# Attention, expert and gated expert on one core: the order of issue set by the kernel's own event list, and attention beside the first expert by whole blocks

## The chip, the core and the metric

One core of a Trainium2 chip runs the whole program. The metric is the device time of one execution in microseconds. TensorE (PE) multiplies, PEld is its weight load, VectorE (DVE), ScalarE (ACT) and GpSimd (POOL) work element by element, SyncE (SP) issues most transfers. Products are summed up in eight banks of 128 x 512 fp32 each.

## What is computed

Attention of 2 batches, 8 heads, 768 positions, 64 values per head, each position seeing 96 positions behind it and 8 global ones; then an expert (silu) of width 2048, then a gated expert of width 1536, over 1536 tokens of 512 values:

```python
scores = scale * np.matmul(q, k.transpose(0, 1, 3, 2)) + bias     # bias: -slope * distance
scores = np.where(keep, scores, -1000000000.0)                    # keep: global or local
a = np.exp(scores - np.max(scores, axis=-1, keepdims=True))
a = a / (np.sum(a, axis=-1, keepdims=True) + 1e-09)
x = np.matmul(a, v)                                               # to tokens x 512
h = x @ w_in
x = (h * (1.0 / (1.0 + np.exp(-h)))) @ w_out
gate = 1.0 / (1.0 + np.exp(-(x @ w_gate)))
out = gate * (x @ w_val) @ w_out2
```

## The kernel before

**Precision.** A product of the experts is made of three on TensorE (`mm3`): each operand is kept as a high and a low part, and high x high, high x low and low x high go into one bank. The weights lie in memory as 64-bit floats. Each tile w0, w1, ... of 128 x 512 weights is loaded raw (`stage`), turned into fp32 in `u` (L156 on ScalarE, a shift L157 and two merges L158 and L161 on VectorE), and cut into its parts (L169 on ScalarE, the subtraction L170 on VectorE). There are 16 tiles w0 to w15 until attention ends, then 24. The tiles come in the order in, in, out, out for each pair of columns of the first expert.

**Attention.** A block is 128 queries of one batch; there are 12, each with four head pairs (`n` counts head pairs). Of a head pair TensorE makes two transposes of queries and keys (`emit_T`, L342, evacuated to `kt` by L353 or L355), the scores (`emit_QK`, L379: 256 columns, or 128 in a batch's first block), four transposes of the probabilities (`emit_PT`, L430, evacuated to `pt` by L434), and PV products (`emit_PV`, L451). Scores and PV are products in fp32, which the trace shows as two records each. In between stand the score operation on VectorE (L394, adds the mask and takes the maximum), the exponentials on ScalarE (L401), two small operations on the sums (L407, L408) and the division, on GpSimd (L413) or, for early blocks, in half on VectorE (L411). When a block's PV is done, `take` writes it to X: the high part by ScalarE (L468), the low part by VectorE (L469). X is cut into three groups x0, x1, x2 of four blocks.

**Stages.** `run_att` does six units of two head pairs, with fillers (bf16 products of a zero tile, L897) put in by hand: 11 ahead, 3 behind each step. `window` runs the rest of attention beside the first expert's first two groups, along `PLAN`: ten entries, each with a pair of columns, a stretch of tokens of a group and a number of attention units (20 in all, two for a block). An entry's products x,w go to banks 5 and 6, the silu makes g (L525, L526, L530 and L532), and its output products g,w are issued during the next entry, into bank 7, evacuated to `acc` by L589 or L591. `phase_rest` does what is left of both experts.

**What sets the order.** A scheduler of the tile framework orders the instructions by its own simulation; from the 16th head pair on, the scores and PV of a unit are tied in the order written. A unit of `att_units` is: scores of two head pairs and PV of the two of a block earlier; then by turns a transpose of probabilities and one of queries and keys. Banks: scores 0 and 1, probabilities 2, PV 3, transposes of queries and keys 4.

Of the kernel before, what the change touches and what calls it, by code (L numbers as in the profile page):

```python
# [11 lines left out]
I32 = mybir.dt.int32  # L12
# [12 lines left out]
TIE = 16  # L25
# [3 lines left out]
N_GLOB = 8  # L29


@with_exitstack
def attn_moe_moe2_kernel(
# [14 lines left out]
    nc = tc.nc  # L48
    B, H, S, D = q.shape
# [15 lines left out]
    stage_p = fast.enter_context(tc.tile_pool(name="stage", bufs=3))  # L65
    u_p = fast.enter_context(tc.tile_pool(name="up", bufs=2))
    g_p = fast.enter_context(tc.tile_pool(name="gp", bufs=4))
    e_p = fast.enter_context(tc.tile_pool(name="ep", bufs=2))
# [10 lines left out]
    nc.gpsimd.memset(pad, 0.0)  # L79
    W = [main.tile([128, 2, 512], F32R, name=f"w{n}") for n in range(16)]  # L80

# [71 lines left out]
    def to_f32(st, raw):  # L153
        lw, hw = raw[:, :, 0], raw[:, :, 1]
        ui = st.bitcast(I32)
        nc.scalar.activation(out=st, in_=hw.bitcast(F32), func=AF.Copy, scale=2.0 ** -112)  # L156
        nc.vector.tensor_scalar(ui, ui, 3, None, op0=ALU.logical_shift_left)  # L157
        nc.vector.scalar_tensor_tensor(  # L158
            out=ui, in0=lw, scalar=29, in1=ui, op0=ALU.logical_shift_right, op1=ALU.bitwise_or
        )  # L160
        nc.vector.scalar_tensor_tensor(  # L161
# [3 lines left out]
    def split_w(n):  # L165
        w = W[n % 24]
        st = u_p.tile([128, 512], F32, tag="u", name="u")
        to_f32(st, stages.pop(n))
        nc.scalar.activation(out=w[:, 0, :], in_=st, func=AF.Copy)  # L169
        nc.vector.tensor_tensor(w[:, 1, :], st, w[:, 0, :].bitcast(F32), ALU.subtract)  # L170

    def load_raw(st, s):
        o = st.rearrange("p f t -> p (f t)")
        if len(s.shape) == 3:
            o = o.rearrange("p (a f) -> p a f", f=256)
        nc.sync.dma_start(out=o, in_=s)

    def dma_w(n):
        st = stage_p.tile([128, 512, 2], I32, tag="stage", name="stage")
# [34 lines left out]
    qk_p = att.enter_context(tc.tile_pool(name="qkp", bufs=2))  # L214
    v_p = att.enter_context(tc.tile_pool(name="vp", bufs=3))
    t_p = att.enter_context(tc.tile_pool(name="tp", bufs=5))
    pt_p = att.enter_context(tc.tile_pool(name="ptp", bufs=3))
# [3 lines left out]
    ssum = [ap1.tile([128, 2], F32, name=f"ssum{i}") for i in range(4)]  # L221

    def load_n():
        raw = ap1.tile([128, 2, 2], I32, name="nraw")
        nc.sync.dma_start(out=raw[:, 0, :], in_=n_global.bitcast(I32).partition_broadcast(128))
        nc.scalar.dma_start(out=raw[:, 1, :], in_=n_local.bitcast(I32).partition_broadcast(128))
        return raw

    def make_n(raw):
        f = ap1.tile([128, 2, 2], F32, name="nf")  # L230
        neg = ap1.tile([128, 2, 1], F32, name="nneg")
        nc.vector.tensor_copy(f, raw)
# [729 lines left out]
```

## Time and profile before

| | us |
|---|---|
| median of 3 runs (682.02 to 682.70) | 682.52 |
| the profiled execution | 681.75 |
| its span in the trace | 680.0 |
| TensorE busy | 667.6 (98%) |
| VectorE busy | 374.2 (55%) |
| ScalarE busy | 277.9 (41%) |
| GpSimd busy | 84.6 (12%) |
| first expert product starts at | 41.40 |
| first product of `phase_rest` that stands alone starts at | 201.11 |

Busy shares are means over stages with different limits. In timeline rows, runs of one kind of instruction stand together; the step from the start of one run to the start of the next is the cost of the run, since the duration printed overlaps the next one's beginning. On VectorE and TensorE alike an instruction's record is longer than its share of the engine. A bracket at the end of a row says how long the engine stood idle ahead of it, and who ended that.

### The profile page before, as it was taken

Reading aid. Unit: us, or ns where it says so; the run is one execution under the profiler, and the core shown is the slowest. Engines: PE = TensorE matmul, PEld = TensorE weight load, DVE = VectorE, ACT = ScalarE, POOL = GpSimd, SP = SyncE. Lnnn points to the kernel's source line nnn. Section 1 sums busy time; section 2 is a strip of 40 time slices with the busy share of each in tenths; the row PEclk is TensorE's granted clock in tenths of the full one; section 3 lists DMA queues with packets and bytes.
Section 4 is the critical chain, followed back from the end, with each engine's and each line's share of the span. In section 5 each row is a group of like instructions: output and inputs, shape, how many; then the busy total and the mean of one; then the engine's idle time right before and its main releaser. Section 6 shows DMA issues by size and latency. Waiting matters only on the chain.

```text
span 680.0 us, 9291 instructions
## 1 busy us (share of the span) xinstructions
PE 667.6 (98%) x3463; PEld 540.1 (79%) x3463; DVE 374.2 (55%) x869; ACT 277.9 (41%) x594; POOL 84.6 (12%) x167
## 2 busy tenths in 40 slices
PE   9999999999999999999999999999999999999996
PEld 7577886777778888888888888888888888888884
DVE  5999975635549999652499941311783311312212
ACT  3797865555546565332366521111452111111110
POOL 4255564343220000000000000000000000000000
PEclk9899999999999999999999999999999999999999
DMA  8666652210004554400025430000250000100101
GB/s 215 174 171 164 171 150 63 48 33 17 17 2 128 182 155 153 125 0 1 24 70 169 141 94 1 0 1 0 63 155 1 1 0 1 62 1 1 62 1 67
DMA packets 65301, 49.05 MB, mean 72 GB/s; under 512 B 39648, under 2 KB 60128, under 8 KB 65248
## 3 DMA queue, kind: packets, MB, share of 16 engines
q1 hardware_dynamic: 64032, 48.11, 24.6%
q8 instruction: 29, 0.48, 0.3%
q10 hardware_dynamic: 1216, 0.26, 0.2%
q14 instruction: 24, 0.20, 0.1%
HBM read 45.22 MB, written 3.15 MB: 71 GB/s over the span
## 4 chain that ended last, share of the span: by engine, by line
PE 93%; DVE 5%; ACT 1%; issue 0%; DVEq 0%
PE bank L505 54%; PE bank L684 14%; PE bank L682 13%; PE bank L379 4%; PE bank L451 3%; PE bank L430 2%; PE bank L897 2%; PE bank L342 1%; DVE t L394 1%; DVE acc L591 1%; DVE w L170 0%; DVE u L158 0%; DVE u L161 0%; DVE acc L703 0%; ACT t L401 0%
## 5 line engine op out<-in xcount | busy, mean ns | idle before, releaser
L505 PE MATMUL bank<-x,w 128*128 128x512 f32 (+1 forms) x1488 | 347.1, 384 | 0.0
L505 PEld LDWEIGHTS bank<-x,w 128*128 128x128 f32 x1488 | 272.6, 188 | 54.4 <-issue 0.8
L542 DVE TENSOR_TENSOR sg<-sg,bank 128x512 f32<-128x512 f32 x36 | 24.7, 687 | 162.5 <-PE bank L505 162.5
L684 PE MATMUL bank<-w,g 128*128 128x512 f32 x432 | 103.9, 389 | 0.0
L684 PEld LDWEIGHTS bank<-w,g 128*128 128x128 f32 x432 | 81.1, 188 | 16.8
L682 PE MATMUL bank<-g,w 128*128 128x512 f32 x384 | 92.4, 389 | 0.0
L682 PEld LDWEIGHTS bank<-g,w 128*128 128x128 f32 x384 | 72.1, 188 | 15.0
L539 ACT ACTIVATE sg<-bank 128x512 f32<-128x512 f32 x36 | 21.6, 599 | 117.3 <-PE bank L505 117.1
L543 ACT ACTIVATE g<-sg 128x512 fp32r<-128x512 f32 x36 | 22.8, 632 | 90.5 <-DVE sg L542 90.5
L156 ACT ACTIVATE u<-stage 128x512 f32<-128x512 f32 x68 | 45.8, 675 | 26.5 <-DVE w L170 26.0
L505 PE MATMUL bank<-g,w 128*128 128x512 f32 (+1 forms) x240 | 53.9, 360 | 2.6 <-DVE acc L591 1.3
L413 POOL TENSOR_SCALAR t<-t,ssum 128x256 f32<-128x256 f32 (+1 forms) x88 | 48.3, 564 | 60.2 <-DVE ssum L408 25.6
L169 ACT ACTIVATE w<-u 128x512 fp32r<-128x512 f32 x68 | 42.5, 629 | 26.2 <-PE bank L505 10.4
L170 DVE TENSOR_TENSOR w<-u,w 128x512 fp32r<-128x512 f32 x68 | 46.9, 692 | 11.4 <-ACT w L169 11.3
L401 ACT ACTIVATE t<-t,nm_all 128x256 f32<-128x256 f32 (+1 forms) x96 | 46.1, 484 | 17.0 <-DVE nm_all L394 17.0
L161 DVE SCALAR_TENSOR_TENSOR u<-stage,u 128x512 int32<-128x512 int32 x68 | 48.2, 709 | 0.3
L158 DVE SCALAR_TENSOR_TENSOR u<-stage,u 128x512 int32<-128x512 int32 x68 | 46.8, 688 | 0.7
L505 PEld LDWEIGHTS bank<-g,w 128*128 128x128 f32 x240 | 38.0, 189 | 10.5 <-DVE acc L591 3.8
L394 DVE CUSTOM_DVE_ANT_0 t<-bank,mask 128x256 f32<-128x256 f32 (+1 forms) x96 | 33.7, 395 | 16.6 <-PE bank L379 15.8
L530 ACT ACTIVATE g<-sg 128x512 fp32r<-128x512 f32 x48 | 30.3, 631 | 22.2 <-DVE sg L529 12.0
L529 DVE SCALAR_TENSOR_TENSOR sg<-sg,bank 128x512 f32<-128x512 f32 x32 | 21.9, 683 | 27.9 <-ACT sg L528 27.9
L528 ACT ACTIVATE sg<-bank 128x512 f32<-128x512 f32 x32 | 19.1, 596 | 39.6 <-PE bank L505 39.2
(91 smaller groups left out, 516.4 us busy)
## 6 DMA issues: line engine op xcount, KB each, us to landing
stage<-in_moe_w_out_dram SPq DMA_DIRECT2D x28, 512.0 KB, 3.6
stage<-in_moe_w_in_dram SPq DMA_DIRECT2D x16, 512.0 KB, 3.7
stage<-in_moe_w_gate_dram SPq DMA_DIRECT2D x12, 512.0 KB, 3.5
stage<-in_moe_w_val_dram SPq DMA_DIRECT2D x12, 512.0 KB, 3.5
v<-in_v_dram SPq DMA_DIRECT2D x12, 256.0 KB, 3.5
out_dram<-acc SPq DMA_DIRECT2D x12, 256.0 KB, 2.0
qk<-in_k_dram SPq DMA_DIRECT2D x11, 256.0 KB, 3.6
qk<-in_q_dram SPq DMA_DIRECT2D x11, 256.0 KB, 3.8
```

Of the source, the lines that this page charges most:

```text
L156: nc.scalar.activation(out=st, in_=hw.bitcast(F32), func=AF.Copy, scale=2.0 ** -112)
L158: nc.vector.scalar_tensor_tensor(out=ui, in0=lw, scalar=29, in1=ui, op0=ALU.logical_shift_right, op1=ALU.bitwise_or)
L161: nc.vector.scalar_tensor_tensor(out=ui, in0=hw, scalar=-2 ** 31, in1=ui, op0=ALU.bitwise_and, op1=ALU.bitwise_or)
L169: nc.scalar.activation(out=w[:, 0, :], in_=st, func=AF.Copy)
L170: nc.vector.tensor_tensor(w[:, 1, :], st, w[:, 0, :].bitcast(F32), ALU.subtract)
L394: nc.vector.tensor_tensor_reduce(t[:, e, 0:w], sp[e], mask[e][:, m0:m0 + w], op0=ALU.add, op1=ALU.min, scale=-c, scalar=3.0e38, accum_out= ...
L401: nc.scalar.activation(out=t[:, e, 0:w], in_=t[:, e, 0:w], func=AF.Exp, scale=-1.0, bias=nm_all[:, gi, 2 * p + e:2 * p + e + 1], accum_out ...
L413: nc.gpsimd.tensor_scalar(t[:, e, 0:w], t[:, e, 0:w], ss[:, e:e + 1], 1.0, op0=ALU.mult, op1=ALU.mult)
L505: nc.tensor.matmul(ps, wl[(slice(None), a) + wsl], xl[(slice(None), b) + xsl], start=(first and j == 0), stop=(last and j == len(order) - 1),)
L530: nc.scalar.activation(out=gt[:, 0, :], in_=sg, func=AF.Copy)
L682: nc.tensor.matmul(yb[d], w[:, a, sl], gt[:, b, :], start=st, stop=en)
L684: nc.tensor.matmul(yb[d], gt[:, a, sl], w[:, b, :], start=st, stop=en)
```

## The change

Operations are no longer handed to the framework at once. `en.tensor`, `en.vector` and so on record them (`Op`) with the regions that they read and write; `link` finds who must come after whom; `order` picks by a list schedule on its own event model (the next engine that can start, among operations that can start within 0.02 us the earliest written), and `issue` hands them over in that order, which the framework keeps. `together` makes a group that isn't broken up. Fillers are put where the model sees TensorE idle before the window. `issue` is called twice: at the window's end and at the end. The tiles of stage, u, g, sg, qk, v, t and pt are fixed rings in place of pools (pt has four in place of three).

In the window, attention goes by whole blocks: `block_units` issues the scores of a block's four head pairs and the PV of the block before as one group, then four transposes of queries and keys, then four of probabilities, spread over the entries of `PLAN`. Banks: scores 0 to 3, probabilities 0 to 3, PV and transposes of queries and keys share 4, outputs 7, then 7 and 4 in the last entry, and 7, 4 and 3 behind the window.

```diff
+SEM = {"tensor": 0.2, "vector": 0.03, "scalar": 0.03, "gpsimd": 0.03, "sync": 0.05}
+TURN = {"fr": 0.095, "fc": 0.097, "tr": 0.095, "tc": 0.097, "rf": 0.192, "cf": 0.148, "rt": 0.247, "ct": 0.203,
+        "rc": 0.195, "cr": 0.147, "tf": -0.082}
...
+    def order(self, filler):
...
+        while any(cand.values()):
+            best = None
+            for e, cs in cand.items():
+                if cs:
+                    at = [(max(free[e], max(m.ready for m in g)), p, i, g) for p, i, g in cs]
+                    s = min(a[0] for a in at)
+                    a = min((a for a in at if a[0] <= s + 0.02), key=lambda a: a[1:3])
+                    if best is None or a[0] < best[0]:
+                        best = a[0], e, a
+            at, e, (_, prio, i, g) = best
+            cand[e].remove((prio, i, g))
+            if e == "tensor" and self.filling:
+                self.filling = not g[0].stop_fill
+                if self.filling:
+                    done += [filler] * max(0, int((at - free[e] - 0.15) / 0.115))
...
+    def issue(self, filler):
+        self.on = False
+        self.link()
+        done = self.order(filler)
+        self.first = len(self.ops)
+        with self.tc.manual_schedule():
+            for o in done:
+                if isinstance(o, Op):
+                    getattr(getattr(self.nc, o.eng), o.meth)(*o.args, **o.kw)
+                else:
+                    o()
...
+    def block_units(b0):
+        def run(b):
+            n = b * NP
+            with en.together():
+                sp = [emit_QK(n + p) for p in range(NP)]
+                for p in range(NP):
+                    emit_PV(n - NP + p)
+            take(n - 1)
+            for p in range(NP):
+                soft(n + p, sp[p], p)
+
+        n = b0 * NP
+        yield lambda n=n: emit_PT(n - 2)
+        yield lambda n=n: emit_T(n + 2)
+        yield lambda n=n: emit_PT(n - 1)
+        yield lambda n=n: emit_T(n + 3)
+        for b in range(b0, NBLK + 1):
+            n = b * NP
+            yield lambda b=b: run(b)
+            for p in range(NP):
+                yield lambda n=n + NP + p: emit_T(n)
+            for p in range(NP):
+                yield lambda n=n + p: emit_PT(n)
...
-            yb = bk["Y"][0]
+            yb = bk["Y"][(d // 2 if two else d) % len(bk["Y"])]
...
+        au_all = list(block_units(n0 * 2 // NP))
+        share, used = 0, 0
         for g, c, n, col0, slots in PLAN:
-            au = list(att_units(n0, n0 + slots))
-            n0 += slots
+            share += slots
+            upto = min(share * (len(au_all) - 1) // (SLOTS - 1), len(au_all))
+            au = au_all[used:upto]
+            used = upto
+            if share == SLOTS:
+                bk["Y"] = [bank[7], bank[4][:, 0:512]]
...
         for j, u in enumerate(att_units(n0, n1)):
             u()
-            warm_up(3)
             unit()
...
         run_att(0, START)
-        bk.update(SA=[bank[0]], SB=[bank[1]], PT=[bank[2]], PV=[bank[3]], T=[bank[4]],
-                  H=[bank[5], bank[6]], Y=[bank[7]])
+        en.stop_fill = True
+        bk.update(SA=[bank[0], bank[2]], SB=[bank[1], bank[3]], PT=bank[0:4], PV=[bank[4]],
+                  T=[bank[4][:, 0:256], bank[4][:, 256:512]], H=[bank[5], bank[6]], Y=[bank[7]])
         prev = window(START)
+        assert not deferred
+        en.issue(filler)
```

First place, VectorE ahead of the second block's write to x0 (u and stage are weight work, t and nm_all scores, kt and ssum attention). Before:

```order
L161 SCALAR_TENSOR_TENSOR u_729<-stage_459,u_729 128x512
L157 TENSOR_SCALAR u_771<-u_771 128x512
L353 TENSOR_SCALAR kt3_131<-bank4_80 128x256
L408 RECIPROCAL ssum1_137<-ssum1_137 128x2
L407 TENSOR_SCALAR ssum2_138<-ssum2_138 128x2
L158 SCALAR_TENSOR_TENSOR u_771<-stage_569,u_771 128x512
L407 TENSOR_SCALAR ssum3_139<-ssum3_139 128x2
L408 RECIPROCAL ssum2_138<-ssum2_138 128x2
L394 ISA t_627,nm_all_92<-bank0_76,mask0_126 128x256
L394 ISA nm_all_92 128x1
L394 ISA t_630,nm_all_92<-bank0_76,mask0_126 128x256
```

The row behind these is the write. After, the rows up to it and the one behind it (every recorded operation stands on L235):

```order
L235 ISA t4_137,nm_all_80<-bank0_64,mask0_113 128x256
L235 ISA nm_all_80 128x1
L235 ISA t4_137,nm_all_80<-bank1_65,mask1_114 128x256
L235 ISA nm_all_80 128x1
L235 TENSOR_TENSOR w2_85<-u0_102,w2_85 128x512
L235 TENSOR_SCALAR ssum2_125<-ssum2_125 128x2
L235 TENSOR_SCALAR u1_103<-u1_103 128x512
L235 RECIPROCAL ssum2_125<-ssum2_125 128x2
L235 TENSOR_TENSOR x0_75<-bank3_67,x0_75 128x4x128
L235 SCALAR_TENSOR_TENSOR u1_103<-stage0_99,u1_103 128x512
```

Before, the sixth weight tile is begun ahead of the write; now the fourth has had its shift alone.

Second place, TensorE in the window, a unit of attention beside expert products (g,w is an output product into bank 7, x,w one of the next entry). Before:

```order
L505 MATMUL bank7_83<-g_944,w7_102 128x256 x3
L379 MATMUL bank0_76<-kt1_129 128x256
L379 MATMUL bank1_77<-kt1_129 128x256
L379 MATMUL bank0_76<-kt0_128 128x256
L379 MATMUL bank1_77<-kt0_128 128x256
L342 MATMUL bank4_80<-ident_84,qk_686 128x128 x2
L505 MATMUL bank5_81<-x0_87,w0_95 128x256
L505 MATMUL bank6_82<-x0_87,w4_99 128x256
L430 MATMUL bank2_78<-ident_84,t_796 128x128 x4
L505 MATMUL bank5_81<-x0_87,w0_95 128x256 x11
```

After, the end of a block's run (eight scores and six PV rows stand ahead of these) and what follows it:

```order
L235 MATMUL bank4_68<-pt0_138,v2_132 64x128 x2
L235 MATMUL bank4_68<-pt0_138,v1_131 64x128 x2
L235 MATMUL bank7_71<-g0_104,w2_85 128x256 x3
L235 MATMUL bank6_70<-x0_75,w4_87 128x256 x3
L235 MATMUL bank7_71<-g0_104,w3_86 128x256 x3
L235 MATMUL bank6_70<-x0_75,w4_87 128x256 x3
L235 MATMUL bank4_68<-ident_72,qk0_128 128x128 x4
L235 MATMUL bank0_64<-ident_72,t0_133 128x128 x4
L235 MATMUL bank4_68<-ident_72,qk0_128 128x128 x4
L235 MATMUL bank6_70<-x0_75,w4_87 128x256 x6
L235 MATMUL bank7_71<-g0_104,w2_85 128x256 x3
```

Transposes into bank 4 now follow twelve expert products behind the PV run that filled it.

Third place, TensorE at the window's end, the output products. Before, all into bank 7:

```order
L505 MATMUL bank7_83<-g_2221,w11_106 128x512 x3
L451 MATMUL bank3_79<-pt_2234,v_1780 64x128 x2
L451 MATMUL bank3_79<-pt_2234,v_1955 64x128 x2
L451 MATMUL bank3_79<-pt_2207,v_1780 64x128 x2
L451 MATMUL bank3_79<-pt_2207,v_1955 64x128 x2
L505 MATMUL bank7_83<-g_2298,w14_109 128x512 x3
L505 MATMUL bank7_83<-g_2304,w15_110 128x512 x3
```

After:

```order
L235 MATMUL bank4_68<-g0_104,w10_93 128x512 x3
L235 MATMUL bank4_68<-g1_105,w11_94 128x512 x3
L235 MATMUL bank7_71<-g2_106,w14_97 128x512 x3
L235 MATMUL bank7_71<-g3_107,w15_98 128x512 x3
L235 MATMUL bank4_68<-g2_106,w14_97 128x512 x3
L235 MATMUL bank4_68<-g3_107,w15_98 128x512 x3
L235 MATMUL bank3_67<-g2_106,w14_97 128x512 x3
L235 MATMUL bank3_67<-g3_107,w15_98 128x512 x3
L235 MATMUL bank7_71<-g2_106,w14_97 128x512 x3
```

The outputs of an entry now stand in a row and change banks.

## Rows read from the trace of the kernel before

**Rows 1.** The page, the chain that ended last, by engine.

```profile
PE 93%; DVE 5%; ACT 1%; issue 0%; DVEq 0%
```

**Rows 2.** Windows: length, busy us and records of each engine; clock, DMA share, GB/s.

```profile
20.00:41.00 21.00, 19.72 (x132) 12.60 (x131) 19.70 (x78) 17.80 (x54) 6.73 (x17) 0.92 0.70 182
50.00:90.00 40.00, 39.07 (x328) 33.35 (x328) 39.93 (x108) 31.90 (x79) 22.33 (x29) 1.00 0.62 167
201.00:673.00 472.00, 472.00 (x2084) 390.64 (x2082) 234.97 (x393) 153.59 (x250) 0.00 (x0) 1.00 0.18 57
```

**Rows 3.** Timeline ahead of the first expert product: start, us, engine, line, operation.

```profile
38.22 0.41 DVE L157 TENSOR_SCALAR u<-u 128x512 int32<-128x512 int32 x1
38.55 0.41 DVE L353 TENSOR_SCALAR kt<-bank 128x256 f32<-128x256 f32 x1
...
39.01 0.68 DVE L158 SCALAR_TENSOR_TENSOR u<-stage,u 128x512 int32<-128x512 int32 x1
39.61 0.15 DVE L407 TENSOR_SCALAR ssum<-ssum 128x2 f32<-128x2 f32 x1
...
39.78 0.42 DVE L394 CUSTOM_DVE_ANT_0 t<-bank,mask 128x256 f32<-128x256 f32 x1
...
40.50 0.69 DVE L469 TENSOR_TENSOR x<-bank,x 128x512 fp32r<-128x512 f32 x1
...
41.40 0.37 PE L505 MATMUL bank<-x,w 128*128 128x256 f32 x1
```

**Rows 4.** Timeline of TensorE ahead of the first scores, at 8.95.

```profile
7.00 2.02 PE L897 MATMUL bank<-warm 128*128 128x256 bf16 x17
```

**Rows 5.** Timeline of TensorE in the window: attention pieces.

```profile
112.35 0.66 PE L451 MATMUL bank<-pt,v 128*64 128x128 f32 x8
112.94 0.44 PE L430 MATMUL bank<-ident,t 128*128 128x128 f32 x2
...
140.38 0.70 PE L379 MATMUL bank<-kt 64*128 64x256 f32 x4
141.01 1.09 PE L451 MATMUL bank<-pt,v 128*64 128x128 f32 x16
...
168.20 0.60 PE L430 MATMUL bank<-ident,t 128*128 128x128 f32 x4
168.56 1.87 PE L505 MATMUL bank<-x,w 128*128 128x512 f32 x7
...
173.56 1.09 PE L451 MATMUL bank<-pt,v 128*64 128x128 f32 x16
174.58 0.66 PE L430 MATMUL bank<-ident,t 128*128 128x128 f32 x4
175.17 1.13 PE L379 MATMUL bank<-kt 64*128 64x256 f32 x8
176.23 0.44 PE L342 MATMUL bank<-ident,qk 128*128 128x128 f32 x2
176.43 1.64 PE L505 MATMUL bank<-g,w 128*128 128x512 f32 x6
```

**Rows 6.** A wait in the timeline; waits of 41 to 201 us: total, times, longest.

```profile
64.61 1.69 PE L505 MATMUL bank<-g,w 128*128 128x256 f32 x12 [0.88 <-DVE acc L589]
...
PEld bank L505 <- DVE acc L591: 3.8, 9, 0.6
```

**Rows 7.** Line L170 up to 100 us: durations, first and last start.

```profile
L170 DVE TENSOR_TENSOR w<-u,w x16: 666/680/886, 19.6 to 87.8; 128x512 fp32r<-128x512 f32 x16
```

**Rows 8.** Timeline: a block's write behind a PV run.

```profile
188.84 0.60 ACT L468 ACTIVATE x<-bank 128x512 fp32r<-128x512 f32 x1 [0.40 <-PE bank L451]
...
189.47 0.69 DVE L469 TENSOR_TENSOR x<-bank,x 128x512 fp32r<-128x512 f32 x1 [0.98 <-ACT x L468]
```

**Rows 9.** Windows with the granted clock ahead of DMA share and GB/s.

```profile
28.66:32.07 3.41, 3.41 (x17) 2.71 (x16) 3.41 (x12) 1.50 (x7) 1.28 (x3) 0.50 0.44 146
104.65:109.33 4.68, 3.68 (x34) 2.49 (x34) 2.81 (x11) 2.52 (x7) 0.57 (x3) 1.00 0.52 112
```

More of the change, by code (lines that the diff above doesn't have):

```diff
@@ L1 @@
[L1 removed]
+from contextlib import ExitStack, contextmanager
+from itertools import cycle
 import concourse.bass as bass
@@ L24 @@
 HA = 8
-TIE = 16
+SLOTS = sum(r[-1] for r in PLAN)
 NEG = 1.0e30
@@ new lines, in region @@
+def region(a):
+    ps, pc = list(a.ap)[0]
+    free = [(st, c) for st, c in list(a.ap)[1:] if c > 1]
+    p0, f0 = (a.offset // ps, a.offset % ps) if ps else (0, a.offset)
+    free.sort(key=lambda e: -abs(e[0]))
+    width = 1
+    while free and abs(free[-1][0]) <= width:
+        st, c = free.pop()
+        width = max(width, (c - 1) * abs(st) + width)
+    runs = [f0]
+    for st, c in free:
+        runs = [r + k * st for r in runs for k in range(c)]
+    return a.name, a.space, p0, p0 + pc, tuple((r, r + width) for r in sorted(runs))
@@ L32, in attn_moe_moe2_kernel, with ring @@
+def ring(pool, shape, dt, name, n):
+    return cycle([pool.tile(shape, dt, name=f"{name}{i}") for i in range(n)])
 @with_exitstack
@@ L307, in load_qk @@
         b, s0 = gi // BLK, gi % BLK * 128
-        t = qk_p.tile([128, 2, H, D], F32, tag="qk", name="qk")
+        t = next(qk_r)
         if gi == 0:
@@ L387, in soft @@
         w = 128 if i == 0 else 256
-        t = t_p.tile([128, 2, 256], F32, tag="t", name="t")
+        t = next(t_r)
         t_t[n] = t
@@ L427, in emit_PT @@
         ps = bk["PT"][n % len(bk["PT"])]
-        for e in range(2):
-            for c in range(nk):
-                nc.tensor.transpose(
-                    ps[:, (e * nk + c) * 128:(e * nk + c + 1) * 128], t[:, e, c * 128:(c + 1) * 128], ident
-                )
-        pt = pt_p.tile([128, 512], F32, tag="pt", name="pt")
-        nc.scalar.activation(out=pt[:, 0:256 * nk], in_=ps[:, 0:256 * nk], func=AF.Copy)
+        with en.together():
+            for e in range(2):
+                for c in range(nk):
+                    en.tensor.transpose(
+                        ps[:, (e * nk + c) * 128:(e * nk + c + 1) * 128], t[:, e, c * 128:(c + 1) * 128], ident
+                    )
+        pt = next(pt_r)
+        en.scalar.activation(out=pt[:, 0:256 * nk], in_=ps[:, 0:256 * nk], func=AF.Copy)
         pt_t[n] = pt
@@ L892, in attn_moe_moe2_kernel, with filler @@
     main2 = {}
-    warm = ap1.tile([128, 256], BF16, name="warm")
-    def warm_up(n):
-        for _ in range(n):
-            nc.tensor.matmul(bank[5][:, 0:256], warm[:, 0:128], warm, start=True, stop=True)
+    def filler():
+        nc.tensor.matmul(
+            bank[5][:, 0:256].rearrange("p (a b) -> p a b", a=2), warm, warm2, start=True, stop=True
+        )
     with ExitStack():
         nc.vector.memset(warm, 0.0)
-        warm_up(11)
+        make_identity(nc, ident)
+        en.begin()
         load_qk(0)
-        make_identity(nc, ident)
         make_iota()
@@ L923, in attn_moe_moe2_kernel @@
         wst["gap"] = 7
+        bk["Y"] = [bank[7], bank[4], bank[3]]
+        en.begin()
         phase_rest(prev)
         flush()
+        en.issue(filler)
     fast.close()
```

515 lines of the change are left out of this document (341 added, 174 removed).

## The prediction

> **What bounds the kernel now.** I read the chain that ended last first: 93% of the span is TensorE and 5% VectorE [rows 1]. That share is a mean, so the busy time by stretches comes next. From 201 us to 673 TensorE has no idle time, and 2084 products in 472.00 us make 0.2265 us for a product of 512 columns [rows 2]. The change issues the same products there on the same weights with VectorE busy for half the stretch, so nothing can come off it. All that can move lies in the first 201 us: the attention start up to the first expert product, and the window in which attention runs beside the first expert. In the start, between 20 and 41 us, VectorE is busy for 19.70 of 21 us, and between 50 and 90 for 39.93 of 40, while TensorE is busy for 39.07 of these 40 [rows 2]. So two engines are nearly full in the window, and a gain on one can stop at the other. Then I read the timeline of VectorE ahead of the first expert product, the timeline of TensorE through attention, and the waits.
>
> **The start.** The first expert product starts at 41.40, right behind VectorE's write of the second attention block at 40.50 + 0.69 [rows 3]. VectorE is busy almost without a break until then, so its order decides. Counted in the two orders ahead of this write: before, 6 shifts of L157, 11 merges of L158 and L161 and 4 subtractions of L170 (weight work), and 18 score operations of 256 columns. After, 4, 6, 3 and 16. Start to start a shift takes 0.33 (38.22 to 38.55), a merge 0.60 (39.01 to 39.61), a score operation about 0.35 (39.78 to 40.50 for two) [rows 3]. I give the subtraction 0.60 too, for it has the merge's size. What leaves the queue ahead of the write is 2 x 0.33 + 5 x 0.60 + 0.60 + 2 x 0.35 = 5.0 us. Against it: 50 fillers stand ahead of the first transpose of queries and keys where about 28 stood. A filler takes about 0.11 (17 in the 1.95 us from 7.00 to 8.95) [rows 4], so the first transpose is about 2.4 later. But before the change TensorE did only fillers from 7.00 until the first score product at 8.95 could start [rows 4], so this slack covers most, and I charge 0.5. The start gives -4.5. Bounds: 0, if it is TensorE's own chain of transposes and products that sets the write, and -5.0.
>
> **Turns on TensorE.** In the window TensorE changes between expert products, score products (kt), transposes and PV products (pt, v). One run of each for two head pairs: PV 173.56 to 174.58 is 1.02, transposes of probabilities 0.59, scores 1.06, transposes of queries and keys 0.20, together 2.87 up to 176.43 [rows 5]. The other two transposes of such a piece stand among expert products: 0.36 (168.20 to 168.56) [rows 5] and, as the row above, 0.20. A piece is 3.43, and a block, two pieces, 6.86. A run has a fixed part: scores for one head pair take 0.63 (140.38 to 141.01) and for two 1.06; PV of one takes 0.59 (112.35 to 112.94) and of two 1.02 [rows 5]. Each further pair costs 0.43. So a whole block in one run costs 1.06 + 2 x 0.43 = 1.92 for scores and 1.02 + 0.86 = 1.88 for PV, and with four transposes of each kind among expert products 4 x 0.36 + 4 x 0.20 = 2.24 the block is 6.04. The gain is 0.82 a block. Nine blocks have both runs in the window, and the last block's PV alone becomes one run from two (-0.16): -7.5. Some work comes into the window that stood ahead of it, for ahead of the first expert product the order has two head pairs of scores (0.86) and two of query transposes (0.40) less, and half a pair of probability transposes (0.18) more: +1.1. Turns give -6.4. Bounds: -7.5 and -4, if every second transpose comes to stand beside an attention run, as it did before at 0.59.
>
> **Waits for bank 7.** All output products of the first expert go through one bank. At 64.61 TensorE waits 0.88 for its evacuation, and weight loads wait 3.8 us in nine other places for the same reason [rows 6]. The new order puts other products between an output and the next one on bank 7, and for the last two groups of outputs turns over banks 7 and 4, then 7, 4 and 3. That gives -4.7; bounds -1 (the 0.88, if weight loads had cover) and -4.7.
>
> **Given back to VectorE.** From the end of the second block's write at 41.2 to the end of the last weight that the window needs, VectorE takes 47.3 us (last subtraction at 87.8, and its 0.68) [rows 7]. In the new order more stands between these two points, counted: 1 shift, 5 merges, 1 subtraction, 2 score operations of 256 columns and 8 of 128, 4 evacuations of kt, 9 small sums, 3 evacuations of bank 7 and 2 block writes. At the prices above, 0.6 for each full-width one, 0.33 for a kt, 0.2 for a narrow score and 0.1 for a small sum, that is 0.3 + 3.0 + 0.6 + 0.7 + 1.6 + 1.3 + 0.9 + 1.8 + 1.2 = 11.4, so 58.7 in all, from 36.7 to about 95.4. TensorE's rows up to the seventh evacuation, with the prices above and about half of 0.2265 for a product of 256 columns, come to some 53 us after the first product at 36.9: 90. TensorE would stand there up to 5.4 us for weights. Some products that need no new weight can stand in the hole, so I charge +4; bounds 0 and +5.4. This takes the place of the start's gain, in part: VectorE's total work is the same, and only its order changes.
>
> **New waits.** PV and the transposes of the next block's queries now share bank 4, so the transposes stand behind the block's write. With idle engines this write takes 1.32 us (ScalarE at 188.84, VectorE's end at 190.16) [rows 8]; queued behind the transposes on TensorE is everything, since its order is fixed. Between a run and its first transpose the order has 12 or 6 products of 256 columns early (1.4 or 0.7 us) and 8 to 9 of 512 later (about 2). With VectorE full in the first half, three or four blocks can lose about 0.5: I charge +2, bounds 0 and +4. Scores in four banks and the fourth pt tile take waits away rather than add them, and since TensorE shows no wait for either in the rows, I cost them at nothing.
>
> **Sum.** -4.5 - 6.4 - 4.7 + 4 + 2 = -9.6 against the profiled execution's 681.75, or 672.2. Its time is 0.77 below the median of the runs shown, 682.52; added back, 672.9.
>
> **The rivals.** *Both costs are covered*: -4.5 - 6.4 - 4.7 = -15.6, 666.9. For it speaks that the new order is planned against engine models with durations close to these rows; against it, VectorE's full 40 us [rows 2]. *VectorE sets the pace until its weights are done* at about 95: then all that is saved earlier is given back, and what is left is turns behind that point (five blocks and the last PV, 4.3) and some 3 of the waits, less 1 for new ones: -6.3, 676.2. *Bank 4 takes it all*: if the write waits in VectorE's queue 1 us longer than I assume in each of nine blocks, +9 cancels the gain: 682. *Slower, by the clock*: between 28.66 and 32.07 the granted clock was 0.50, that is 1.2 GHz in place of 2.4, after a stretch with only scores and transposes and a wait [rows 9]. That cost half of 3.41, 1.7 us. A whole block now runs 3.8 us of scores and PV with no expert product between. If each of nine such runs brought one fall, it would cost 15.3 and the time would be 688; it decides from the sixth fall on. Against it: from 104.65 to 109.33 there is almost only attention on TensorE and 1.00 us without work, and the clock stayed at 1.00 [rows 9].
>
> The Trainium skill, "TensorE: Matmul & The Clock Gate", section "A second HAM failure mode: psum-queue depth-cycling", says that going round several accumulation banks can leave small gaps between groups of products, and that the clock then swings between its two levels. By that rule the new rings of banks would be what brings the falls, and the time would be the slower rival's; the trace shows one fall in 200 us, at a wait, and none where bank 7 was waited for, so it stays a rival with a small chance.
>
> That the order isn't kept is hardly possible: the operations are issued in it, and the two listings of the kernels show it.
>
> **How the numbers follow.** Forecast 672.9: 0.48. All gains 666.9: 0.13. VectorE's pace 676.2: 0.18. Cancelled, about 682: 0.09. Clock, 688: 0.12. A measurement of this kernel can tell 0.2%, 1.4 us, from no change. The first three are faster, 0.79; the fourth is the same, with half its spread: 0.08 and a little of it slower, so slower is 0.13. The range runs from 665.5, a little under the full gain, to 680.5, where VectorE and bank 4 both cost their upper bounds (start -4.5, turns -4, the waits -3, then +5.4 and +4: -2.1, 680.4). It leaves out the last two cases.
>
> **What would show it.** Right: the first expert product at about 37; no TensorE wait on the evacuation of bank 7 above 0.3; runs of scores of about 1.9 and of PV of about 1.9 in one piece; VectorE full until about 95; the window's end near 191 in place of 201; from there the same 472 us. Wrong: a first product later than 40 (TensorE set the start, not VectorE); a transpose of queries that waits over 1 us for the block's write in most blocks; a granted clock under 1.00 in the window; or TensorE idle in many small pieces that no single releaser explains, which would say that the planner's durations are off and a fixed order can't fill holes.

## The result: 8.8 us faster, and where they come from

The changed kernel takes 673.86 us (median of 4 runs, 672.87 to 674.41) against 682.61 for the kernel before; the ratio is 0.987, 95% interval 0.9853 to 0.9887. The forecast was 672.9 within 665.5 to 680.5. The profiled execution took 674.26 with a span of 672.5; the two profiled executions differ by 7.5. Rows and sums below are of profiled executions, verdicts of medians.

The page of the changed kernel: busy time by engine, and the chain that ended last ([rows 1] of before).

```profile
PE 654.9 (97%) x3462; PEld 539.6 (80%) x3462; DVE 372.6 (55%) x869; ACT 277.4 (41%) x594; POOL 83.1 (12%) x167
PE 88%; DVE 8%; ACT 2%; issue 1%; POOL 0%; DVEq 0%; ACTq 0%
```

TensorE's share of the chain fell from 93% to 88% and VectorE's rose from 5% to 8%: TensorE has less to do, and waits more. The windows (length, busy us and records of PE, PEld, DVE, ACT, POOL; clock, DMA share, GB/s), as [rows 2]:

```profile
33.00:37.00 4.00, 4.00 (x31) 3.05 (x28) 3.17 (x14) 2.84 (x8) 1.67 (x6) 0.57 0.57 158
...
50.00:60.00 10.00, 9.04 (x81) 8.22 (x82) 9.24 (x22) 7.80 (x17) 3.18 (x6) 1.00 0.70 204
60.00:70.00 10.00, 8.83 (x84) 7.87 (x79) 9.82 (x32) 8.47 (x25) 6.89 (x12) 1.00 0.56 140
90.00:191.00 101.00, 99.16 (x666) 79.58 (x664) 55.44 (x193) 59.01 (x159) 39.98 (x75) 1.00 0.18 46
200.00:656.00 456.00, 456.00 (x2014) 377.48 (x2013) 229.00 (x382) 148.32 (x244) 0.00 (x0) 1.00 0.19 59
```

The first row is for later. The last row is as before, 456.00 / 2014 = 0.2264 us a product: nothing moved there. In the first half of the window TensorE now has 1 us of idle time in 10 with VectorE nearly full. TensorE's timeline at the start ([rows 3, 4]):

```profile
0.97 7.96 PE L1167 MATMUL bank<-warm 128*128 128x256 bf16 x50 [0.97 <-DVE warm L1172]
8.77 0.38 PE L235 MATMUL bank<-ident,qk 128*128 128x128 f32 x2
...
31.37 0.44 PE L235 MATMUL bank<-ident,qk 128*128 128x128 f32 x2 [1.48 <-DVE kt L235]
...
33.73 1.97 PE L235 MATMUL bank<-pt,v 128*64 128x128 f32 x16
...
37.10 1.32 PE L235 MATMUL bank<-x,w 128*128 128x256 f32 x9
```

The first expert product starts at 37.10 in place of 41.40. Attention's runs in the window ([rows 5]):

```profile
57.44 2.00 PE L235 MATMUL bank<-kt 64*128 64x256 f32 x16
59.36 1.97 PE L235 MATMUL bank<-pt,v 128*64 128x128 f32 x32
61.72 0.44 PE L235 MATMUL bank<-ident,t 128*128 128x128 f32 x2 [0.39 <-POOL t L235]
...
112.40 2.00 PE L235 MATMUL bank<-kt 64*128 64x256 f32 x16
114.32 1.97 PE L235 MATMUL bank<-pt,v 128*64 128x128 f32 x32
116.22 1.65 PE L235 MATMUL bank<-x,w 128*128 128x512 f32 x6
```

A block's scores take 1.92 and its PV 1.90 start to start. TensorE's waits from 37 to 195 us (waited for; total, times, longest; [rows 6]):

```profile
PE bank L235 <- DVE x L235: 1.3, 3, 0.5
PE bank L235 <- DVE acc L235: 0.9, 2, 0.5
PE bank L235 <- POOL t L235: 0.9, 2, 0.5
PE bank L235 <- DVE kt L235: 0.9, 3, 0.5
PE bank L235 <- DVE w L235: 0.6, 1, 0.6
PE bank L235 <- ACT kt L235: 0.4, 2, 0.2
PE bank L235 <- ACT w L235: 0.3, 1, 0.3
PE bank L235 <- ACT t L235: 0.3, 1, 0.3
```

These 5.6 us are idle time as the trace prints it. Counted as the excess of each start over the steps of undisturbed runs, which takes in the slower restart behind a wait, they come to some 8.7 us from the first expert product on, against some 6.1 before: weights 1.2, probabilities 1.6, transposes of queries and keys 2.1 on the block's write and 2.1 on the evacuation of kt, bank 7 1.3, and 0.3 of small ones.

One split serves for the kernels compared below: the start of the first expert product, the start of the last run of 36 output products, and the length between. First the last run of before and of the changed kernel, then the windows between the two starts:

```profile
664.87 8.32 PE L684 MATMUL bank<-w,g 128*128 128x512 f32 x36
656.88 8.32 PE L235 MATMUL bank<-w,g 128*128 128x512 f32 x36
...
41.40:664.87 623.47, 620.16 (x3161) 506.50 (x3160) 338.20 (x727) 250.97 (x512) 68.67 (x118) 1.00 0.22 64
37.10:656.88 619.78, 614.10 (x3171) 508.08 (x3170) 340.98 (x744) 254.75 (x525) 68.26 (x120) 1.00 0.22 66
```

| profiled execution | first expert product | last run of 36 | length between | median us |
|---|---|---|---|---|
| before | 41.40 | 664.87 | 623.47 | 682.61 |
| changed | 37.10 | 656.88 | 619.78 | 673.86 |
| pairs | 36.00 | 661.72 | 625.72 | 677.56 |
| one_y_bank | 36.74 | 658.98 | 622.24 | 675.96 |
| light_weights | 37.11 | 654.62 | 617.51 | 671.31 |
| few_fillers | 35.17 | 654.82 | 619.65 | 671.65 |
| hole_fill | 33.73 | 654.51 | 620.78 | 670.97 |
| half_runs | 33.70 | 658.91 | 625.21 | 675.99 |

So the change took 4.3 us off the start and 3.7 off what follows: TensorE is busy for 6.1 less there (614.10 for 620.16) and idle for 2.4 more. The end, behind the last run's start, is 0.5 longer.

### The profile page after: what moved, and what is told of

It reads as the page before. It is cut to its first block, busy times and chain, and to the rows that moved or that the text cites. A ratio compares the mean times of both kernels' runs of the same rounds, so it can differ in the third digit from the quotient of the medians.

```text
span 672.5 us, 9377 instructions
## 1 busy us (share of the span) xinstructions
PE 654.9 (97%) x3462; PEld 539.6 (80%) x3462; DVE 372.6 (55%) x869; ACT 277.4 (41%) x594; POOL 83.1 (12%) x167
## 4 chain that ended last, share of the span: by engine, by line
PE 88%; DVE 8%; ACT 2%; issue 1%; POOL 0%; DVEq 0%; ACTq 0%
PE bank L235 87%; DVE t L235 2%; DVE u L235 2%; PE bank L1167 1%; ACT t L235 1%; DVE acc L235 1%; DVE x L235 1%; DVE ssum L235 1%; DVE w L235 1%; DVE kt L235 0%; ACT kt L235 0%; DVE nm_all L235 0%; POOL t L235 0%; DVE sg L235 0%; ACT x L235 0%
## 5 line engine op out<-in xcount | busy, mean ns | idle before, releaser
L235 PE MATMUL bank<-x,w 128*128 128x512 f32 (+1 forms) x1488 | 348.2, 384 | 0.6 <-DVE w L235 0.6
L235 PEld LDWEIGHTS bank<-x,w 128*128 128x128 f32 x1488 | 272.0, 188 | 54.0 <-DVE w L235 0.8
L235 PE MATMUL bank<-g,w 128*128 128x512 f32 (+1 forms) x624 | 146.1, 377 | 1.5 <-DVE acc L235 0.9
L235 PEld LDWEIGHTS bank<-g,w 128*128 128x128 f32 x624 | 110.8, 188 | 24.1 <-DVE acc L235 1.6
L235 ACT ACTIVATE sg<-bank 128x512 f32<-128x512 f32 x84 | 50.0, 595 | 161.1 <-PE bank L235 159.1
L235 DVE TENSOR_TENSOR sg<-sg,bank 128x512 f32<-128x512 f32 x36 | 24.7, 687 | 161.6 <-PE bank L235 161.6
L235 PE MATMUL bank<-w,g 128*128 128x512 f32 x432 | 103.4, 389 | 0.0
L235 ACT ACTIVATE g<-sg 128x512 fp32r<-128x512 f32 x84 | 53.0, 631 | 105.6 <-DVE sg L235 105.5
L235 PEld LDWEIGHTS bank<-w,g 128*128 128x128 f32 x432 | 81.1, 188 | 16.8
L235 DVE SCALAR_TENSOR_TENSOR u<-stage,u 128x512 int32<-128x512 int32 x136 | 93.2, 693 | 1.7
L235 DVE TENSOR_TENSOR g<-sg,g 128x512 fp32r<-128x512 f32 x68 | 46.9, 690 | 23.4 <-ACT g L235 23.0
L235 ACT ACTIVATE u<-stage 128x512 f32<-128x512 f32 x68 | 45.7, 674 | 32.5 <-DVE w L235 24.0
L235 ACT ACTIVATE w<-u 128x512 fp32r<-128x512 f32 x68 | 42.6, 629 | 30.6 <-DVE u L235 16.2
L235 DVE SCALAR_TENSOR_TENSOR sg<-sg,bank 128x512 f32<-128x512 f32 x48 | 32.8, 683 | 38.5 <-ACT sg L235 38.4
L235 POOL TENSOR_SCALAR t<-t,ssum 128x256 f32<-128x256 f32 (+1 forms) x88 | 48.3, 563 | 44.7 <-DVE ssum L235 38.8
L235 ACT ACTIVATE t<-t,nm_all 128x256 f32<-128x256 f32 (+1 forms) x96 | 45.9, 480 | 15.8 <-DVE nm_all L235 14.2
L235 DVE TENSOR_TENSOR w<-u,w 128x512 fp32r<-128x512 f32 x68 | 46.2, 685 | 11.1 <-ACT w L235 10.9
L235 DVE TENSOR_TENSOR acc<-acc,bank 128x512 f32<-128x512 f32 x48 | 32.2, 685 | 18.7 <-PE bank L235 18.6
L235 DVE CUSTOM_DVE_ANT_0 t<-bank,mask 128x256 f32<-128x256 f32 (+1 forms) x96 | 33.6, 396 | 9.0 <-PE bank L235 8.8
L235 DVE TENSOR_SCALAR u<-u 128x512 int32<-128x512 int32 x68 | 28.7, 425 | 5.2 <-ACT u L235 4.4
L235 ACT ACTIVATE pt<-bank 128x512 f32<-128x512 f32 (+1 forms) x48 | 26.3, 556 | 12.2 <-PE bank L235 12.0
L235 PE MATMUL bank<-ident,t 128*128 128x128 f32 x176 | 27.5, 278 | 0.9 <-POOL t L235 0.9
```

The source lines that it names most:

```text
L235: getattr(getattr(self.nc, o.eng), o.meth)(*o.args, **o.kw)
```

## The experiments

**The order alone.** `pairs` keeps the list order and goes back to two head pairs a unit, with before's banks, so that all outputs go to bank 7 too. (Notes behind a # in the cuts of code below were put in for this text.)

```diff
-            au = au_all[used:upto]
+            au = list(att_units(n0, n0 + slots))
...
-        bk.update(SA=[bank[0], bank[2]], SB=[bank[1], bank[3]], PT=bank[0:4], PV=[bank[4]],
-                  T=[bank[4][:, 0:256], bank[4][:, 256:512]], H=[bank[5], bank[6]], Y=[bank[7]])
+        bk.update(SA=[bank[0]], SB=[bank[1]], PT=[bank[2]], PV=[bank[3]], T=[bank[4]],
+                  H=[bank[5], bank[6]], Y=[bank[7]])
```

> The changed kernel with attention in the window by two head pairs as before (scores in banks 0 and 1, probabilities in 2, PV in 3, transposes of queries and keys alone in 4, all outputs in bank 7), still issued in the order of the kernel's own event list. Theory (the sum of terms): the start stays as in the changed kernel, first product at about 37; the whole-block gain of 6.4 is lost, the waits of transposes on the block's write and on each other in bank 4, 4.3 us in the changed kernel's trace, go too, and one bank for outputs costs 1 to 2: 677, between 676 and 679, with scores in runs of 1.06. Rival, the order alone makes the gain and whole blocks nothing: 674. Rival, whole blocks are all of it and the order nothing: 682.

677.56, ratio 0.9926 (0.991 to 0.9941). Of the 8.8 us the order alone makes 5, all at the start (36.00): from there on it is 2.3 longer than before (625.72 against 623.47). TensorE's waits there (first row), and one of them in its timeline:

```profile
PE bank L235 <- ACT pt L235: 3.9, 8, 1.0
...
49.27 0.63 PE L235 MATMUL bank<-ident,t 128*128 128x128 f32 x4 [0.71 <-ACT pt L235]
```

With one bank for all probabilities, a transpose waits for the evacuation of the one before, and in a fixed order nothing else goes first. Whole blocks and their banks make the other 3.7: from the first product on they are 5.9 shorter than `pairs` (619.78 for 625.72), 4.3 of it time in which TensorE is busy (614.10 for 618.43), but their first product comes 1.1 later. In `pairs` the list put ten fillers ahead of that product, between 29 and 33 us, and the granted clock is 1.00 there; the changed kernel has none there, and its clock falls. The time is in the theory's range, though the start wasn't to change and the 3.9 us of waits weren't foreseen. Neither rival holds.

**The bank ring.** `one_y_bank` leaves the window's outputs in bank 7 to the end.

```diff
-            if share == SLOTS:
-                bk["Y"] = [bank[7], bank[4][:, 0:512]]
...
-        bk["Y"] = [bank[7], bank[4], bank[3]]
```

> The changed kernel with all outputs of the window in bank 7 to its end. Theory: the outputs that now stand in a row behind 186 us would each wait for the evacuation, some 0.6 us as at 191.54 and 197.00 before, for six to eight of them less what the order can put between: 1.5 to 4 us longer, 675.5 to 678. Rival, the list order finds other products to put between them at no cost: 674.

675.96 (ratio 0.9904, 0.9889 to 0.9919), 2.1 above the changed kernel, in the theory's range. TensorE's timeline at the window's end:

```profile
193.79 1.66 PE L235 MATMUL bank<-g,w 128*128 128x512 f32 x6 [0.78 <-DVE acc L235]
...
196.32 1.60 PE L235 MATMUL bank<-g,w 128*128 128x512 f32 x6 [0.87 <-DVE acc L235]
```

The order found other products for all but two of these outputs, and these two make most of what the ring saves: 1.65 us of idle time.

**VectorE's share.** `light_weights` leaves out 24 merges, both of each of the tiles w4 to w15.

```diff
+        if light:            # 4 <= n < 16
+            return
```

> The changed kernel with the two merges on VectorE left out for the twelve weight tiles w4 to w15, some 14 us less work for VectorE in the window; the output is not the reference's. Theory, VectorE's queue causes most of what was given back (weights 1.2, late probabilities 1.6, kt evacuations 2.1, all released by VectorE or behind it): waits fall from 8.7 to under 4, 669 to 671. Rival, sharing bank 4 causes it: waits of the queries' transposes on the block's write and on kt stay, 4 of the 8.7, and the time is 672 to 673.

671.31 (ratio 0.9834, 0.9819 to 0.9849), 2.5 below the changed kernel. TensorE's waits:

```profile
PE bank L235 <- DVE kt L235: 1.7, 5, 0.5
PE bank L235 <- DVE x L235: 1.6, 3, 1.0
```

The waits for probabilities are gone and those for weights nearly so (0.2); those of the transposes in bank 4 stay, and grow from 1.3 and 0.9 to 1.6 and 1.7. The time is between the two expectations, and the cause is both: taking this work off VectorE is worth 2.5 us, and most of the waits that are left stand at bank 4.

**The fillers ahead of the first transpose.** `few_fillers` has 28, as before.

```diff
-                    done += [filler] * max(0, int((at - free[e] - 0.15) / 0.115))
+                    k = max(0, int((at - free[e] - 0.15) / 0.115))
+                    done += [filler] * (min(k, 28) if not self.lane[0] else k)
```

> The changed kernel with 28 fillers ahead of the first transpose, as before, in place of 50. The first transpose should start at about 6.2 in place of 8.77. Theory (VectorE's queue sets the start): most of it waits again for the mask and the first kt evacuation, first expert product 0.5 earlier or less, 673.4 to 673.9. Rival, the start is a chain of transposes, scores and PV on TensorE: first expert product 1.3 to 2.4 earlier, 671.5 to 672.6.

671.65 (ratio 0.9843, 0.983 to 0.9857): 2.2 below the changed kernel, the rival. The timeline of TensorE, and a window:

```profile
0.97 4.71 PE L1168 MATMUL bank<-warm 128*128 128x256 bf16 x28 [0.97 <-DVE warm L1173]
5.52 0.38 PE L236 MATMUL bank<-ident,qk 128*128 128x128 f32 x2
...
8.58 0.49 PE L236 MATMUL bank<-kt 64*128 64x128 f32 x4 [1.06 <-DVE kt L236]
...
31.60:34.60 3.00, 3.00 (x23) 2.65 (x22) 2.87 (x13) 2.05 (x6) 0.84 (x4) 0.50 0.58 178
```

The operands of the first transpose were there at least 3.3 us before the changed kernel uses them (5.52 for 8.77); the planner thought them later and filled the time. Of this 1.9 reach the first expert product (35.17), and the rest goes mostly in a wait for kt (1.06), which stands behind the making of the mask on VectorE. My theory for this run was wrong.

**The hole and the clock.** In the last row above the granted clock is 0.50 (1.2 GHz), behind a stretch of 4.6 us in which TensorE stood idle for 2 and did only some transposes and scores. `hole_fill` adds 12 and 4 fillers there.

```diff
+        if n == 13:
+            en.ops[-2].fill = 12      # in emit_T; in emit_QK 4 for n == 10
```

> few_fillers with 12 fillers ahead of the transpose that waits 1.48 us for a kt evacuation ahead of the first expert product, and 4 ahead of the scores behind it. In few_fillers the granted clock is 0.50 from 31.6 to 34.6 there, with scores, PV and transposes at half speed. Theory: the hole brings the fall, the fall lies on the chain to the first expert product, and without it this product starts about 1.2 earlier: 670.4, clock 1.00 from 27 to 37. Rival, VectorE sets the first product anyway: 671.6, clock 1.00 all the same. Rival, the fall has another cause: clock 0.50 as before, 671.6.

670.97 (ratio 0.9834, 0.9818 to 0.985), the lowest median of all, though its interval overlaps with that of few_fillers. The same window, the timeline of TensorE behind it, and VectorE's write of the second block:

```profile
31.60:34.60 3.00, 2.52 (x28) 2.04 (x27) 2.97 (x13) 2.89 (x10) 0.96 (x4) 1.00 0.83 227
...
33.73 0.38 PE L238 MATMUL bank<-x,w 128*128 128x256 f32 x1
34.83 1.21 PE L238 MATMUL bank<-x,w 128*128 128x256 f32 x8 [0.71 <-DVE x L238]
...
34.10 0.67 DVE L238 TENSOR_TENSOR x<-bank,x 128x512 fp32r<-128x512 f32 x1
```

The clock stays at 1.00, so in this place the hole was what brought the fall. The other traces agree: of the orders that wait for this kt, all five without fillers beside the wait fall (the changed kernel, one_y_bank, light_weights, few_fillers, t_late), and none of the seven with fillers does (pairs, hole_fill, half_runs and the four orders below that start from hole_fill). But not every idle stretch brings a fall, as kt_first shows below. The first product, which needs the high part alone, is 1.44 earlier, but the next waits for VectorE's write until 34.83. Here VectorE sets the start, and of the 1.44 only 0.3 are left at the last run.

**Moving the waits about.** Five more orders, on few_fillers (the first two) or hole_fill, and two of them together:

```diff
             for p in range(NP):
-                yield lambda n=n + NP + p: emit_T(n)
-            for p in range(NP):
                 yield lambda n=n + p: emit_PT(n)
+                yield lambda n=n + NP + p: emit_T(n)             # t_late
...
+        en.bias = -400                                           # kt_first, around evac() and the block's write
...
-            if n % 2:
+            if n % 2 and n < 12:                                 # kt_scalar
...
-        wst["gap"] = 7
+        wst["gap"] = 6                                           # gap6
...
-                  T=[bank[4][:, 0:256], bank[4][:, 256:512]],
+                  T=[b[:, 0:256] for b in bank[0:4]],            # t_in_pt_banks, transposes one step behind t_late's
```

> few_fillers with each block's transposes of queries and keys behind its transposes of probabilities, by turns, in place of ahead of all four; the first now stands behind 15 expert products and a transpose of probabilities in place of 12 products. Theory, the waits of these transposes (2.1 on the block's write and 2.1 on the evacuation of kt in few_fillers) come from their place right behind a PV run into the same bank: most of the 4.2 go, 668 to 669.5. Rival, VectorE is what is late in the first half and the wait moves to the next in line (probabilities, scores): 671 to 672.

671.14 (ratio 0.9829, 0.9813 to 0.9844), the rival. The profiled execution is 1.6 us above the median of its runs, and its granted clock over the whole span is 0.991, where three of the five have 0.999. Its timeline of TensorE in the first half of the window, and the window with its clock:

```profile
53.64 0.97 PE L236 MATMUL bank<-g,w 128*128 128x256 f32 x6 [1.71 <-DVE acc L236]
54.54 3.17 PE L236 MATMUL bank<-kt 64*128 64x256 f32 x16
57.64 2.43 PE L236 MATMUL bank<-pt,v 128*64 128x128 f32 x32
...
53.60:59.60 6.00, 5.96 (x50) 4.80 (x52) 4.85 (x23) 4.21 (x15) 2.08 (x3) 0.72 0.46 158
```

A wait of 1.71 us for bank 7 has come up, and behind it the clock falls in a whole-block run, which then takes 5.5 us in place of 3.8. That is the price of the slower rival, 1.7, once, and not in every execution: 1.7 us of 671 is 0.0025, so at 0.999 neither this fall nor the one ahead of the first product came in full, in the same order.

> few_fillers with the evacuations of kt and the block's write ahead of everything else in the list where both could start. Theory, these waits come from the order on VectorE and ScalarE, with scores and weights ahead of them: of the 4.2 us about half go, 669.5 to 670.5. Rival, in the model they already go as soon as they can, and the lists differ too little to matter: 671.4 to 671.9.

673.80 (ratio 0.9873, 0.9855 to 0.9891), slower than few_fillers by 2.1, outside both expectations. What was put behind in the lists made new waits: 1.97 us for an exponential on ScalarE at 61.15 and 1.23 for an evacuation of bank 7 at 53.22.

```profile
61.15 0.95 PE L236 MATMUL bank<-g,w 128*128 128x256 f32 x6 [1.97 <-ACT t L236]
```

Behind this wait the granted clock stayed at 1.00, so an idle stretch as long as those of the falls need not bring one. The profiled execution is the fastest of its four (672.76), so not all of the 2.1 is seen in it; the two slowest have a granted clock of 0.994 and 0.995 for its 0.997.

> hole_fill with all evacuations of kt from the fourth block on made by ScalarE, in place of every second by VectorE: some 18 x 0.33 = 6 us less for VectorE in the window, 18 x 0.35 more for ScalarE. Theory, VectorE is what gives the start's gain back up to 100 us: its waits (weights 0.9 + 0.8 + 0.5, probabilities 1.6, kt 1.5) fall by about a third, 669 to 670. Rival, ScalarE, busy for 8 of 10 us there, becomes late in its place: 671 to 672.

672.31 (ratio 0.9854, 0.9838 to 0.9871). The time is the rival's or a little over, but not for its reason: waits for ScalarE's kt are 0.9 in all. TensorE waits longer for the block's write, 3.3 us in seven places where hole_fill waits 2.0 in four (in each, one of them is the first expert product, the others transposes into bank 4), and a weight is late by 1.1.

> hole_fill with the weight tiles of the attention start issued every 6 steps in place of 7, so that more weight work stands ahead of the second block's write on VectorE. Theory, VectorE's total work up to 100 us sets the pace and only its order changes: the first expert product comes 0.5 to 1 later, the waits for weights at 34.83 and 45.07 (1.7 together) go, and the time is the same within 0.5, 670.5 to 671.4. Rival, the start is worth its full size at the end: 671.5 to 672.

672.31 (ratio 0.986, 0.9844 to 0.9877), the rival's time and beyond it. The first product is later, as meant, but waits for the block's write grow to 2.8 and for probabilities from 0.9 to 1.8; only the wait for weights (0.2) is nearly gone.

> Both edits: the early weights and the kt evacuations on ScalarE. Theory: 668.5 to 670, the better of the two or a little under. Rival, ScalarE becomes late: 671 to 672.

671.91 (ratio 0.9851, 0.9834 to 0.9867), the rival's time, but again not for its reason: waits for the block's write are 4.3 us in six places, for ScalarE's kt 0.8. The longest, in TensorE's timeline:

```profile
59.38 0.66 PE L238 MATMUL bank<-ident,qk 128*128 128x128 f32 x4 [1.78 <-DVE x L238]
```

Behind it the granted clock falls once more (0.57 from 60.4 to 64.4), beside expert products this time; the profiled execution (673.14) is the slowest of its four.

> hole_fill with the transposes of queries and keys in banks 0 to 3, each in the bank of a transpose of probabilities just evacuated, so that bank 4 holds PV alone. Theory, sharing bank 4 with the block's write makes 2.1 us of waits, most of them behind 89 us where VectorE is no longer full: these go, 668.5 to 669.5. Rival, the waits move, since the transposes now come later and nearer to the scores that need kt: 670.5 to 672.

671.78 (ratio 0.9838, 0.9825 to 0.9852), the rival's time, with half of the theory in it. TensorE's waits behind 62 us and ahead of it, and a window:

```profile
PE bank L238 <- ACT pt L238: 0.3, 1, 0.3
...
PE bank L238 <- ACT pt L238: 2.8, 3, 1.1
...
57.00:60.60 3.60, 3.60 (x18) 2.63 (x18) 3.60 (x11) 1.36 (x3) 0.52 (x2) 0.54 0.61 142
```

Behind 62 us nearly no idle time is left (the first row is all; hole_fill has 2.3 us there). The later place of the transposes alone doesn't do that, for t_late still waits 1.6 for the block's write behind 62 us, so sharing bank 4 made the waits there. Ahead of it the transposes now wait for evacuations of probabilities, 2.8 us (second row), and behind such waits the clock falls once, at half speed for most of 3.6 us. That takes back what the second half gained.

**The price of a turn.** `half_runs` cuts each block's run in two.

```diff
-                sp = [emit_QK(n + p) for p in range(NP)]
-                for p in range(NP):
+                sp = [emit_QK(n + p) for p in (h, h + 1)]        # run(b, 0), then run(b, 2)
+                for p in (h, h + 1):
                     emit_PV(n - NP + p)
```

> hole_fill with each block's run cut in two (scores and PV of two head pairs, twice), the banks, the order of the rest and the start unchanged. Theory, a turn has the price of the prediction's rows, 0.2 for a run of scores, 0.16 for one of PV and 0.1 to 0.2 for entering and leaving, so 0.4 to 0.55 for each of nine blocks: 3.6 to 5 longer, 674.5 to 676. Rival, TensorE waits for others anyway, and a longer list of its own is hidden in these waits: 671 to 672.5.

675.99 (ratio 0.9906, 0.9891 to 0.9921), 5.0 above hole_fill, the theory. Two half runs in its timeline of TensorE:

```profile
120.53 1.14 PE L238 MATMUL bank<-kt 64*128 64x256 f32 x8
121.60 1.09 PE L238 MATMUL bank<-pt,v 128*64 128x128 f32 x16
122.62 0.96 PE L238 MATMUL bank<-x,w 128*128 128x512 f32 x3
123.51 1.13 PE L238 MATMUL bank<-kt 64*128 64x256 f32 x8
124.58 1.09 PE L238 MATMUL bank<-pt,v 128*64 128x128 f32 x16
125.60 0.97 PE L238 MATMUL bank<-x,w 128*128 128x512 f32 x3
```

Twice 2.09 is 4.18, where a whole run takes 3.82 (112.40 to 116.22 above): 0.36. The three products between take 0.89 in place of 0.68: 0.21 for leaving and entering. Nine blocks by 0.57 are 5.1. Between the two profiled executions it is 4.4 (the last runs start at 658.91 and 654.51), with TensorE busy for 4.2 more from the first product on and idle about as long, so it is turns and not waits; in one of the nine blocks the halves came to stand side by side, without the 0.21.

## Why the prediction was right, step by step

**Start: -4.5 forecast, -4.3 measured, by errors that cancel; that the number fits is luck.** The step "this slack covers most, and I charge 0.5" failed: the 22 more fillers cost 1.9 at the first expert product (few_fillers). In a fixed order the whole chain hangs on its first transpose, and a slack of TensorE in the kernel before was no slack here, for by then other things were earlier too. And a fall of the clock, from 33 to 37 (0.57 in the mean of the first window shown), lay on the chain, which I had priced only inside the window; without it the first product comes 1.4 earlier (hole_fill). Against both, the order gave VectorE more than the 5.0 counted, which was also the bound: with fillers and fall out of the way its write ends at 34.77 (34.10 + 0.67 in hole_fill) in place of 41.19, 6.4 earlier, and the second expert product starts with it.

**Turns: -6.4 forecast, -6.1 measured** as TensorE's busy time from the first expert product to the last run (614.10 for 620.16), so the size is borne out. The runs have the lengths that the sum used (1.92 and 1.90 for 1.92 and 1.88), and cutting them costs 5.0. Of the 6.1, some 4.3 is turns between runs (4.3 by pairs, 4.2 by half_runs); 1.7 came with the list order, for pairs has it already (618.43 for 620.16). The same step at fixed banks, 0.57 a block, is under the 0.82 of the forecast, which also took in the transposes that stood between a run of PV and one of scores at 0.59.

**Bank 7: -4.7 forecast.** Counted as excess of starts, waits for it fell from 5.3 to 1.3, so -4.0; of idle time as the trace prints it, only from 2.2 to 0.9. The ring alone is 2.1 of it (one_y_bank), the order the rest. As 3.8 us of weight loads' waits were only partly TensorE's idle time, the size was a little over.

**Given back: +4 to VectorE and +2 to bank 4 forecast, +2.8 and +4.2 measured** as excess of starts (weights 1.2 and probabilities 1.6; transposes 2.1 and 2.1). The sum, +6, was under by 1, since the first was too high by 1.2 and the second too low by 2.2. The two are partly exchanged: in light_weights, with less work on VectorE, the waits at bank 4 grow. I had not counted the second wait, of a transposed pair on the evacuation of kt from the same half bank two pairs earlier.

**The rest.** After the first expert product the forecast was -5.1 and -3.7 came; the end took 0.5 more. With 0.2 at the start that makes 2.1 in the profiled execution (674.26 against 672.2 in the sum). The medians differ by only 1.0, 673.86 against 672.9, since the 0.77 added at the end of the sum for the median has the other sign here: the changed kernel's median lies 0.4 under its profiled execution. Of the signs named, the first product at 37, the runs of 1.9 in one piece and the same 0.2264 us a product in the long last stage came true. Two waits for bank 7 of 0.5 are over the 0.3 named, VectorE is full until about 90 in place of 95 (busy for 5.00 of 5 us up to 90, for 3.77 of the next 5), and the 5.6 us of idle time lie in fifteen pieces with eight kinds of releaser. That comes near the last sign of being wrong, durations of the planner that are off, and few_fillers shows one that was. The window's end can't be named: the list order mixes its last outputs, up to 199.89, with products of the next stage. The rival "bank 4 takes it all" had the right mechanism at half its price, and the slower rival's clock falls did come inside the window in three of the experiments (t_late, gap6_kt_scalar, t_in_pt_banks), once each, at some 1.7. The rule of the Trainium skill weighed there, "TensorE: Matmul & The Clock Gate", section "A second HAM failure mode: psum-queue depth-cycling", isn't borne out in this kernel: the window of the changed kernel uses these rings at a granted clock of 1.00 throughout, and the falls in the window of other orders stand behind waits of 1.1 to 1.8 us.

What stays open: why the clock fell behind some waits and not behind others as long; and which of VectorE's and ScalarE's operations would have to go first to take the waits that are left ahead of 60 us. The orders tried moved them, and one that takes those behind 60 us (t_in_pt_banks) paid for it ahead.

## What to carry to other kernels

A fixed order is only as good as the planner's durations at its start: operands believed 3 us late cost 2.1 us at the last run, and nothing that came later could take it back, so compare the first operations of a planned order with the trace first. Long runs of one kind pay by the number of turns they save, some 0.5 us for a run of scores and PV here, and this can be priced from two runs of different length. When one engine is full and another fixed behind it, shifting single operations moves the waits; take work off the full engine, or fill the hole where a trace shows a slower clock behind it.

## What the runs showed of the hardware

In these traces the granted clock fell to its lower level (0.50, 1.2 GHz) behind stretches in which TensorE had idle time next to transposes, scores, PV and a few expert products: 2.0 us of 4.6 in few_fillers at 31 us, 1.7 of 2.1 in t_late at 54, 1.9 of 3.0 in t_in_pt_banks at 57, 1.8 of 5.4 in gap6_kt_scalar at 60, but only 0.7 of 3.7 in the kernel before ahead of its fall at 28.66 ([rows 9]). Such a stretch didn't bring a fall each time: kt_first stood idle for 1.97 us up to 61.15 and stayed at 1.00, and the five executions of t_late have granted clocks between 0.991 and 0.999 with one and the same order. 16 fillers in the stretch of few_fillers kept the clock at 1.00. Whole-block runs of 3.8 us without an expert product did not bring a fall by themselves: from 37 us on the changed kernel's trace shows none until TensorE's last product.
